# One tile for each PSUM bank, and VectorE for the two-operand work of the Strassen phases, in a kernel of attention and two feed-forward layers

## The chip, the cores and the metric

The kernel runs on one core of a Trainium2 chip, in float32. The metric is the device time of one execution in microseconds (us); the time of a kernel is the median of its runs.

## What is computed

Windowed attention over 4 x 8 heads of 768 tokens gives x of 3072 tokens by 512 features. Two feed-forward layers follow:

```python
# _moe_ref: layer 1                      # _moe2_ref: layer 2
h = x @ w_in      # 512 -> 2048          h = x @ w_in
relu6 = np.clip(h + 3.0, 0.0, 6.0)       g = np.maximum(0.01 * h, h)
g = h * relu6 / 6.0                      return g @ w_out
return g @ w_out  # 2048 -> 512
```

The inputs of the layers' weights are 64-bit floats; the kernel decodes them to 32-bit ones itself.

## The kernel before, in words

Every float32 operand is held as a high and a low part, and a product is the sum of three: high x high, low weight x high, high x low. A "low part" is a subtraction of two SBUF operands (`minus`, line 284), after the cast that makes the high part (`copy`, line 281). A matmul is 128 x 128 by 512 columns and takes one bank of PSUM.

The tokens are 6 blocks of 512. In layer 1 each block has 16 hidden blocks f (`hidden`, 12 matmuls) and 16 outputs (`output`, 12 matmuls into four banks, one for each 128 features of the result), in the order h(f+1), y(f). The outputs of layer 1 go to DRAM (`spill`).

In layer 2 the hidden products are made by Strassen's method (Winograd's form) on pairs p of blocks (2p, 2p+1) and pairs i of hidden blocks (2i, 2i+1): seven products instead of eight, each of 6 matmuls, with sums of operands before and sums of results after. `x_pair` and `x_quarter` form the right operands of a pair from `spill` (b11, t1 to t4 and others, two quarters of 11 VectorE or GpSimd operations each), `w_set` the left ones of an i (s1 to s4) from weights in DRAM, loaded into `wm`, which has two buffers; `through_dram` sends the decoded `w_out` of layer 2 through the same two buffers. `seven` makes one product and what follows from it. The order of an iteration i is products 1, 6, 5, 7, an output, products 2, 3, 4, an output; the outputs are of block 2p, from the i before. Products 2, 3 and 4 accumulate in the banks of 1, 5 and 7. The results for block 2p are used at once (`two_parts` makes g of them); those for block 2p+1 go to DRAM (`later`) and come back (`again`) when the stage is done, for an output stage of 15 or 16 outputs of block 2p+1. So there are three Strassen stages with an output stage behind each.

PSUM has eight banks. Before the change `ya` and `yb` are tiles of two banks, `h` is one of two tiles of one bank, `at` is a tile of two. Outputs and products of a stage have either `ya`, `yb` or `h`, `h`, `at`, in turn: `banks_of` gives four (tile, half) pairs. In the first and last Strassen stage products 1 and 6 write the two `h`, product 5 `at[0]`, product 7 `at[1]`, and the outputs `ya`, `yb`; in the middle stage products 1, 6, 5, 7 write `ya[0]`, `ya[1]`, `yb[0]`, `yb[1]`.

The order of all instructions is made by a planner in Python, `schedule`. A task has a key (its place in the order of TensorE's work), the engines that may do it with a cost for each, the tasks it follows, the buffers it allocates and uses. Whenever an engine is free, the planner gives it the ready task of least key and emits its instructions; a second engine of a task takes it only when the first has more than 2500 ns more to do (`SLACK`). Its costs for 512 columns are 602 ns for VectorE and 1225 for GpSimd. TensorE's products form one chain (`product`), so their order is fixed. A product is emitted in three parts of two matmuls; what reads its result is emitted some 575 ns after its planned end (`SEM` and `MARGIN`). The semaphore waits are put in afterwards by the framework, tile by tile, from the order in which the instructions were emitted. DMAs are issued by SyncE's queue, in order.

Lines that matter: 281 `copy`, 284 `minus`, 630 `hidden`'s matmuls, 684 `output`'s, 877 `seven`'s, 894 `plus` in `seven`, 905 the leak, 925 and 927 what follows product 2, 830 the sums of `w_set`, 372 and 814 the loads into `wm`, 908 and 943 the stores to `later` and the loads from it.

Of the kernel before, what the change touches and what calls it, by code (L numbers as in the profile page):

```python
# [9 lines left out]
F32 = mybir.dt.float32  # L10
# [25 lines left out]
N = 512  # L36
# [169 lines left out]
def tile_attn_moe_moe2(ctx: ExitStack, tc: tile.TileContext, raw, w1i, w1o, w2i, w2o, out):  # L206
# [15 lines left out]
    pools = {t: (ctx.enter_context(tc.tile_pool(name=t, bufs=k[0])), k[1], k[2]) for t, k in KINDS.items()}  # L222
    for y in "ab":
        pools[f"y{y}"] = (ps_y, [128, 2, 512], F32)
# [5 lines left out]
    def make(b, kind=None):  # L230
        pool, shape, dt = pools[b.tag]
# [420 lines left out]
    def banks_of(other):  # L652
        if other:
            t = Buf("at")
            return [(Buf("h"), None), (Buf("h"), None), (t, 0), (t, 1)]
        a, b = Buf("ya"), Buf("yb")
        return [(a, 0), (a, 1), (b, 0), (b, 1)]

    def bank(b):
        b, i = b  # L660
        t = made(b)
        return t if i is None else t[:, i]

    def output(lay, j, f, c0, n):
# [7 lines left out]
        banks = ybuf[lay, j]  # L672
        ys = list(dict.fromkeys(b for b, _ in banks))
        g, w = gbuf[lay, j, f, c0], wbuf[lay + "o", f]
# [30 lines left out]
    def y_out(lay, j, f, t0, n, d, y, k, two):  # L705
        s = Buf("ys")
        key = pos_y[lay, j, f] - 12
        scale = 1.0 / 6.0 if lay == "1" else 1.0
        dst = (out if lay == "2" else spill)[d, :, t0:t0 + n]
        if two and f < KF - 1:  # L710
            dst = half[j, d]

        def take(e):
            if e == "ACT":
                nc.scalar.mul(make(s)[:, :n], bank(y)[:, :n], scale)
            else:
                nc.vector.tensor_scalar(out=make(s)[:, :n], in0=bank(y)[:, :n], scalar1=scale, scalar2=None, op0=ALU.mult)

        def plus(e):
            nc.vector.scalar_tensor_tensor(out=s.t, in0=bank(y), scalar=scale, in1=s.t, op0=ALU.mult, op1=ALU.add)  # L720

        if two and f == KF - 1:
            l = add(lambda e: nc.sync.dma_start(out=make(s), in_=half[j, d]), {"SP": dma(n * 512)}, key - 8, after=[yhalf[j, d], *firsts], allocs=[s])
            k = add(plus, {"DVE": dve(n)}, key, after=[k, l], uses=[s, y[0]])
        else:
            k = add(take, {"DVE": dve(n)} if d % 2 else {"ACT": act(n, 50.0)}, key, after=[k], allocs=[s], uses=[y[0]])
# [22 lines left out]
    def x_quarter(p, j, key, need):  # L749
# [13 lines left out]
        def sub(out, x, y, after, allocs=(), uses=()):  # L763
            return add(lambda e: minus(e, out(), x(), y()), {"DVE": dve(N), "POOL": pool(N)}, key, after=after, allocs=allocs, uses=uses)

        def parts_of(name, of, own, after):
            bufs = xop[p, name]
            first = xtask[p, name][0][:1], xtask[p, name][1][:1]
            hi = add(lambda e: copy(e, operand(p, name, 0, j).bitcast(F32R), of()), {"ACT": act(N), "DVE": dve2(N)}, key, after=after + first[0], allocs=[] if first[0] else bufs[:1], uses=[own] + (bufs[:1] if first[0] else []))
            new = not first[1] and len(bufs) == 2  # L770
            lo = add(lambda e: minus(e, operand(p, name, 1, j).bitcast(F32R), of(), operand(p, name, 0, j).bitcast(F32)), {"POOL": pool(N), "DVE": dve(N)}, key, after=[hi] + first[1], allocs=bufs[1:] if new else [], uses=[own, bufs[0]] + ([] if new else bufs[1:]))
            xtask[p, name][0].append(hi)
# [19 lines left out]
        d11 = parts_of("b11", at("b11"), src["b11"], [got["b11"]])  # L792
        t1 = add(t_1, {"DVE": dve(N), "POOL": pool(N)}, key, after=[got["b11"], got["b12"]], allocs=[tt], uses=[src["b11"], src["b12"]])
        t2 = sub(t_at(1), at("b22"), t_at(0), [t1, got["b22"]], uses=[tt, src["b22"]])
# [11 lines left out]
    def w_set(p, i, key):  # L806
# [19 lines left out]
        def form(out, x, y, op, after, allocs=(), uses=()):  # L826
            def fn(e):
                for b in allocs:
                    make(b, ([128, 512], F32))
                engine(e).tensor_tensor(out=part(out), in0=part(x), in1=part(y), op=op)  # L830
            return add(fn, {"DVE": dve(256), "POOL": pool(256)}, key, after=after, allocs=allocs, uses=[*raws, *uses])

# [5 lines left out]
        def two(t, src, n, after):  # L838
# [7 lines left out]

            hi = add(fn_hi, {"ACT": act(n), "DVE": dve2(n)}, key + 0.5, after=after + gate, allocs=[ts[t]], uses=[src])
            lo = add(fn_lo, {"POOL": pool(n), "DVE": dve(n)}, key + 0.6, after=[hi], uses=[src, ts[t]])
            return hi, lo
# [6 lines left out]
    def seven(p, i, n):  # L856
# [32 lines left out]

        def plus(out, x, y, opts, after, allocs=(), uses=()):  # L890
            def fn(e):
                for q in allocs:
                    make(q, ([128, 2, N], F32) if q is ut else None)
                engine(e).tensor_tensor(out=out(), in0=x(), in1=y(), op=ALU.add)  # L894
            return add(fn, opts, key, after=after, allocs=allocs, uses=uses)

        def take(q, b, after, allocs=()):
            def fn(e):
                for x in allocs:
                    make(x, ([128, 2, N], F32))  # L900
                copy(e, ut.t[:, q], bank(b))
            return add(fn, {"ACT": act(N, 50.0), "DVE": dve(N)}, key, after=after, allocs=allocs, uses=[b[0]] + ([] if allocs else [ut]))

# [5 lines left out]

        low = {"POOL": pool(N), "DVE": dve(N)}  # L910
        dv = {"DVE": dve(N)}
        if n == 1:
            done[1] = take(0, b1, [k], allocs=[ut])
        elif n == 6:
            done[6] = plus(lambda: ut.t[:, 0], lambda: bank(b2), lambda: ut.t[:, 0], dv, [k, done[1]], uses=[ut, b2[0]])
        elif n == 5:
            done[5] = take(1, b3, [k, done[1]])
        elif n == 7:
            done[7] = plus(lambda: ut.t[:, 1], lambda: bank(b5), lambda: ut.t[:, 1], dv, [k, done[5]], uses=[ut, b5[0]])
            r = Buf("ys")  # L920
            q = plus(lambda: r.t, lambda: ut.t[:, 0], lambda: ut.t[:, 1], {"POOL": pool(N), **dv}, [done[7], done[6]], allocs=[r], uses=[ut])
            put(r, f2, leak(r, q))
        elif n == 2:
            r = Buf("r")
            q = add(lambda e: nc.scalar.mul(make(r), bank(b1), 0.01), {"ACT": act(N, 50.0)}, key, after=[k, *rs[-1:]], allocs=[r], uses=[b1[0]])
            rs.append(q)
            q = add(lambda e: nc.vector.tensor_tensor(out=r.t, in0=bank(b1), in1=r.t, op=ALU.max), dv, key, after=[q], uses=[r, b1[0]])
# [129 lines left out]
```

## Time and profile before

| | before |
|---|---|
| median of 3 runs | 1195.41 us (1194.85 to 1195.47) |
| profiled execution, its own time | 1192.55 us |
| its span in the profile | 1190.8 us |
| granted clock of TensorE, mean | 0.987 |
| last matmul ends | 1185.87 us, 4.93 us ahead of the end |
| attention and layer 1 | to about 627.7 us |
| first Strassen stage and its output stage | 627.68 to 769.57, to 813.07 us |
| middle Strassen stage and its output stage | 813.07 to 961.66, to 1004.44 us |
| last Strassen stage and its output stage | 1004.44 to 1185.87 us |

How to read it: times are us from the start of the span. PE is TensorE, DVE VectorE, ACT ScalarE, POOL GpSimd, SP SyncE's queue. A matmul's end in the profile is modelled, and matmuls overlap, so a busy share of PE is no measure of its speed: the rate of a stretch is its matmuls over its time. A VectorE instruction of 0.69 us is followed by the next about 0.60 us after its start when nothing holds that up.

### The profile page before, as it was taken

To read this page: it belongs to the slowest core of one execution; us is meant where nothing else is said; L and a number is where in the kernel's file an instruction comes from. 1 tells how busy PE (TensorE), PEld (TensorE's weight loads), DVE (VectorE), ACT (ScalarE), POOL (GpSimd) and SP (SyncE) were. 2 spreads that over 40 slices of the span, in tenths; PEclk is the share of its full clock that TensorE was granted. 3 is DMA by queue.
4 is the path that set the end of the run, shared out by engine and by line. 5 is a ranking of instruction groups with operands and counts; after the bars stand their busy time and mean duration, and the time that the engine had idled before them with its cause. 6 is when DMAs were issued, how large, how long until landed. Compare 5 with 4: busy or idle time off the path is not lost.

```text
span 1190.8 us, 19604 instructions
## 1 busy us (share of the span) xinstructions
PE 1111.6 (93%) x7632; PEld 897.2 (75%) x7632; DVE 625.4 (53%) x988; ACT 472.5 (40%) x1154; POOL 387.7 (33%) x319
## 2 busy tenths in 40 slices
PE   4599999999999999999999999899888899999998
PEld 3487888888888888888887777677666677777776
DVE  5789975554435535415517666744544571655310
ACT  4557655445554544433324333333222332322222
POOL 1030000011232232125524443664344474444343
PEclk9699999999999999999999999899999999999999
DMA  8894454654445534321103332622121260311150
GB/s 195 256 244 143 144 152 131 180 158 134 139 140 149 138 96 131 97 62 53 36 1 115 98 104 101 209 82 80 62 62 54 74 235 19 99 61 62 38 184 36
DMA packets 85341, 135.50 MB, mean 114 GB/s; under 512 B 8448, under 2 KB 41216, under 8 KB 85248
## 3 DMA queue, kind: packets, MB, share of 16 engines
q1 hardware_dynamic: 85248, 134.25, 37.3%
q8 instruction: 60, 0.98, 0.4%
q14 instruction: 33, 0.27, 0.1%
HBM read 98.57 MB, written 35.65 MB: 113 GB/s over the span
## 4 chain that ended last, share of the span: by engine, by line
PE 83%; DVE 5%; ACT 3%; DMA 3%; issue 3%; POOL 2%; SPq 2%; POOLq 0%; DVEq 0%; ACTq 0%
PE h L630 21%; PE ya L684 15%; PE yb L684 15%; PE at L877 7%; PE h L877 5%; PE h L684 5%; PE at L684 5%; PE yb L877 4%; PE ya L877 3%; ACT w L281 2%; PE at L506 1%; DMA w<-in_w1i 1%; DMA w<-in_raw 1%; PE at L445 1%; DVE ys L894 1%
## 5 line engine op out<-in xcount | busy, mean ns | idle before, releaser
L284 POOL TENSOR_TENSOR g<-r,g 128x512 fp32r<-128x512 f32 x108 | 143.2, 1326 | 463.3 <-ACT g L281 459.2
L684 PE MATMUL ya<-g,w 128*128 128x512 f32 x864 | 266.8, 394 | 4.8 <-ACT g L281 2.1
L684 PE MATMUL yb<-g,w 128*128 128x512 f32 x864 | 264.2, 391 | 0.0
L630 PE MATMUL h<-xh,w 128*128 128x512 f32 x768 | 195.5, 395 | 1.9 <-ACT xh L281 1.9
L684 PEld LDWEIGHTS ya<-g,w 128*128 128x128 f32 x864 | 160.8, 188 | 41.0 <-ACT g L281 3.5
L684 PEld LDWEIGHTS yb<-g,w 128*128 128x128 f32 x864 | 163.1, 189 | 34.8
L630 PEld LDWEIGHTS h<-xh,w 128*128 128x128 f32 x768 | 144.2, 190 | 33.1 <-ACT xh L281 3.1
L646 DVE SCALAR_TENSOR_TENSOR r<-r,h 128x512 f32<-128x512 f32 x96 | 65.9, 686 | 171.7 <-ACT r L643 171.6
L281 ACT CAST g<-r 128x512 fp32r<-128x512 f32 x144 | 89.7, 623 | 158.2 <-DVE r L646 51.4
L643 ACT ACTIVATE r<-h,three 128x512 f32<-128x512 f32 x96 | 66.6, 693 | 155.6 <-PE h L630 155.1
L630 PE MATMUL h<-xl,w 128*128 128x512 f32 x384 | 104.4, 394 | 0.6 <-issue 0.6
L684 PE MATMUL h<-g,w 128*128 128x512 f32 x288 | 89.8, 396 | 1.5 <-DVE g L284 1.0
L684 PE MATMUL at<-g,w 128*128 128x512 f32 x288 | 89.1, 394 | 0.0
L877 PE MATMUL at<-w 128*128 128x512 f32 x288 | 74.9, 398 | 14.9 <-DVE ys L894 9.4
L630 PEld LDWEIGHTS h<-xl,w 128*128 128x128 f32 x384 | 72.2, 189 | 16.2 <-issue 1.0
L284 POOL TENSOR_TENSOR g<-w,g 128x512 fp32r<-128x512 f32 x45 | 60.3, 1340 | 55.3 <-ACT g L281 55.3
L877 PEld LDWEIGHTS at<-w 128*128 128x128 f32 x288 | 52.5, 188 | 33.1 <-DVE ys L894 14.5
L684 PEld LDWEIGHTS h<-g,w 128*128 128x128 f32 x288 | 54.8, 191 | 14.6 <-DVE g L284 1.5
L281 ACT CAST g<-w 128x512 fp32r<-128x512 f32 x48 | 29.8, 621 | 85.9 <-PE at L684 55.8
L684 PEld LDWEIGHTS at<-g,w 128*128 128x128 f32 x288 | 54.9, 191 | 11.9
L284 DVE TENSOR_TENSOR w<-st,w 128x512 fp32r<-128x512 f32 x28 | 35.9, 1294 | 48.7 <-ACT w L281 48.7
L284 POOL TENSOR_TENSOR w<-wm,w 128x512 fp32r<-128x512 f32 (+1 forms) x44 | 54.8, 1250 | 8.6 <-ACT w L281 6.7
(163 smaller groups left out, 1502.0 us busy)
## 6 DMA issues: line engine op xcount, KB each, us to landing
wm<-w322i SPq DMA_DIRECT2D x48, 256.0 KB
later<-ys SPq DMA_DIRECT2D x48, 256.0 KB
w<-later SPq DMA_DIRECT2D x24, 512.0 KB
a<-in_raw SPq DMA_DIRECT2D x44, 224.0 KB
w<-in_w1i SPq DMA_DIRECT2D x16, 512.0 KB
w<-in_w1o SPq DMA_DIRECT2D x16, 512.0 KB
w<-in_w2i SPq DMA_DIRECT2D x16, 512.0 KB
w<-in_w2o SPq DMA_DIRECT2D x16, 512.0 KB
```

The costliest lines, as they stand in the source:

```text
L281: nc.scalar.copy(out, in_) if e == "ACT" else engine(e).tensor_copy(out=out, in_=in_)
L284: engine(e).tensor_tensor(out=out, in0=a, in1=b, op=ALU.subtract)
L445: nc.tensor.matmul(ps.t[h * CHUNK:(h + 1) * CHUNK, par, i * W:(i + 1) * W], qk[h // 2].t[r, gp, (h % 2) * G + c * CHUNK:(h % 2) * G + (c + ...
L506: nc.tensor.matmul(pv.t[(h % 2) * D:(h % 2 + 1) * D, par, (h // 2) * 2 * G + i * CHUNK:(h // 2) * 2 * G + (i + 1) * CHUNK], v[h // 2].t[r, ...
L630: nc.tensor.matmul(h.t[:, :n], w.t[:, 1 if p == 1 else 0, k * 128:(k + 1) * 128], x[:, k, c0:c0 + n], start=(p == 0 and k == 0), stop=(p = ...
L643: nc.scalar.activation(out=make(r)[:, :n], in_=h.t[:, :n], func=AF.Relu, bias=three[:, 0:1], scale=1.0)
L646: nc.vector.scalar_tensor_tensor(out=r.t[:, :n], in0=r.t[:, :n], scalar=6.0, in1=h.t[:, :n], op0=ALU.min, op1=ALU.mult)
L684: nc.tensor.matmul(bank(banks[d])[:, c0:c0 + n], w.t[:, 1 if p == 1 else 0, d * 128:(d + 1) * 128], g.t[:, 1 if p == 2 else 0, :n], start= ...
L877: nc.tensor.matmul(bank(to), t.t[:, 1 if q == 1 else 0, o, kt * 128:(kt + 1) * 128], operand(p, name, 1 if q == 2 else 0, kt).bitcast(F32R ...
L894: engine(e).tensor_tensor(out=out(), in0=x(), in1=y(), op=ALU.add)
```

## The change

Each of the eight banks gets a tile of its own. `ya` and `yb` become four tiles `y`; `at` becomes, when attention is done, two tiles `hx`; before the first output, where units of attention had `ya` and `yb`, they have tiles `ab` and `ac`, whose pool is closed when the first `y` is made. `banks_of` gives four tiles.

In `x_quarter`, `w_set`, `seven`, `again` and for the g of layer 2 the choice of engine goes: every subtraction and sum is VectorE's, every cast of a high part there ScalarE's. `split_w` and `hidden` keep theirs (GpSimd makes layer 1's low parts of g from the third block on).

After the products the sums are ordered anew. Before: U2 = P1 + P6 (P1 copied by ScalarE), P5 copied by ScalarE, P5 + P7 with P7 in PSUM, and then U2 + (P5 + P7), both in SBUF, by GpSimd or VectorE. After: U3 = P5 + U2 with P5 in PSUM, then P7 + U3 with P7 in PSUM, both by VectorE.

```diff
-    ps_y = ctx.enter_context(tc.tile_pool(name="ps_y", bufs=1, space=PSUM))
     ps_h = ctx.enter_context(tc.tile_pool(name="ps_h", bufs=2, space=PSUM))
-    ps_a = ctx.enter_context(tc.tile_pool(name="ps_a", bufs=1, space=PSUM))
+    begin = ctx.enter_context(ExitStack())
+    ps_b = begin.enter_context(tc.tile_pool(name="ps_b", bufs=1, space=PSUM))
+    attention = ctx.enter_context(ExitStack())
+    ps_a = attention.enter_context(tc.tile_pool(name="ps_a", bufs=1, space=PSUM, side="right"))
...
-    places |= {"ya": 1, "yb": 1, "h": 2, "at": 1}
+    places |= {"ab": 1, "ac": 1, "y": 4, "h": 2, "at": 1, "hx": 2}
...
+        if b.tag in ("hx", "y") and b.tag not in pools:
+
+            (attention if b.tag == "hx" else begin).close()
...
     def banks_of(other):
-        if other:
-            t = Buf("at")
-            return [(Buf("h"), None), (Buf("h"), None), (t, 0), (t, 1)]
-        a, b = Buf("ya"), Buf("yb")
-        return [(a, 0), (a, 1), (b, 0), (b, 1)]
+        return [Buf(t) for t in (("h", "h", "hx", "hx") if other else "yyyy")]
...
-            hi = add(lambda e: copy(e, operand(p, name, 0, j).bitcast(F32R), of()), {"ACT": act(N), "DVE": dve2(N)}, key, after=after + first[0], allocs=[] if first[0] else bufs[:1], uses=[own] + (bufs[:1] if first[0] else []))
+            hi = add(lambda e: copy(e, operand(p, name, 0, j).bitcast(F32R), of()), {"ACT": act(N)}, key, after=after + first[0], allocs=[] if first[0] else bufs[:1], uses=[own] + (bufs[:1] if first[0] else []))
...
-            lo = add(fn_lo, {"POOL": pool(n), "DVE": dve(n)}, key + 0.6, after=[hi], uses=[src, ts[t]])
+            hi = add(fn_hi, {"ACT": act(n)}, key + 0.5, after=after + gate, allocs=[ts[t]], uses=[src])
+            lo = add(fn_lo, {"DVE": dve(n)}, key + 0.6, after=[hi], uses=[src, ts[t]])
...
-        low = {"POOL": pool(N), "DVE": dve(N)}
-        dv = {"DVE": dve(N)}
+        low = {"DVE": dve(N)}
...
-            done[5] = take(1, b3, [k, done[1]])
+            done[5] = plus(lambda: ut.t[:, 1], lambda: bank(b3), lambda: ut.t[:, 0], [k, done[6]], uses=[ut, b3])
         elif n == 7:
-            done[7] = plus(lambda: ut.t[:, 1], lambda: bank(b5), lambda: ut.t[:, 1], dv, [k, done[5]], uses=[ut, b5[0]])
             r = Buf("ys")
-            q = plus(lambda: r.t, lambda: ut.t[:, 0], lambda: ut.t[:, 1], {"POOL": pool(N), **dv}, [done[7], done[6]], allocs=[r], uses=[ut])
-            put(r, f2, leak(r, q))
+            done[7] = plus(lambda: r.t, lambda: bank(b5), lambda: ut.t[:, 1], [k, done[5]], allocs=[r], uses=[ut, b5])
+            put(r, f2, leak(r, done[7]))
...
-        two_parts("2", 2 * p + 1, f, r, k, key, {"POOL": pool(N), "DVE": dve(N)}, f % 2)
+        two_parts("2", 2 * p + 1, f, r, k, key, {"DVE": dve(N)}, f % 2)
...
-        unit(u // 2, u % 2, -80.0 + 6.0 * u, ("at", "ya", "yb", "at")[u], own=u < 3, direct=True)
+        unit(u // 2, u % 2, -80.0 + 6.0 * u, ("at", "ab", "ac", "at")[u], own=u < 3, direct=True)
```

## Rows read from the trace of the kernel before

**Rows 1.** The page: busy us (share of the span) and instructions of each engine.

```profile
PE 1111.6 (93%) x7632; PEld 897.2 (75%) x7632; DVE 625.4 (53%) x988; ACT 472.5 (40%) x1154; POOL 387.7 (33%) x319
```

**Rows 2.** Chain of waits in order of time (start, us, what), one iteration, first stage.

```profile
640.90 2.72 PE h L877 x12
643.62 1.83 PE at L877 x8
...
645.47 0.59 ACT w L281
...
653.24 0.70 DVE ys L894
...
657.93 2.72 PE h L877 x12
```

**Rows 3.** Waits of TensorE, 560 to 1190: who for whom: us, times, longest.

```profile
PE at L877 <- ACT w L281: 10.9, 16, 0.8
PE at L877 <- DVE ys L894: 9.4, 12, 0.8
PE yb L877 <- DVE ys L894: 6.7, 7, 2.0
PE yb L877 <- ACT w L281: 5.4, 8, 0.7
PE ya L877 <- ACT w L281: 5.3, 7, 0.8
```

**Rows 4.** Busy us (instructions) by stage: stretch, us, engines, granted clock, DMA, GB/s.

```profile
627.68:769.57 141.89, 129.30 (x542) 101.64 (x541) 98.62 (x130) 53.39 (x97) 66.78 (x50) 0.98 0.37 123
769.57:813.07 43.50, 42.16 (x182) 34.18 (x181) 15.40 (x15) 14.79 (x26) 26.73 (x20) 0.98 0.26 84
813.07:961.66 148.59, 131.02 (x541) 100.70 (x541) 80.30 (x119) 41.21 (x75) 65.74 (x50) 0.99 0.26 85
961.66:1004.44 42.78, 41.42 (x181) 33.63 (x181) 15.64 (x15) 14.27 (x25) 25.81 (x19) 1.00 0.28 100
1004.44:1185.87 181.43, 170.53 (x732) 135.89 (x731) 73.28 (x106) 45.55 (x80) 74.73 (x59) 1.00 0.23 77
```

**Rows 5.** Waits of TensorE again, of the last stretch alone, 1004.44 to 1185.87.

```profile
PE at L877 <- DVE ys L894: 5.5, 7, 0.8
PE at L877 <- ACT w L281: 5.4, 8, 0.7
```

**Rows 6.** Timeline of TensorE, end of the first stage: start, us, what [idle before <-releaser].

```profile
763.13 0.73 PE L684 MATMUL ya<-g,w 128*128 128x512 f32 x2 [1.77 <-ACT g L281]
764.94 2.07 PE L684 MATMUL ya<-g,w 128*128 128x512 f32 x4 [1.07 <-POOL g L284]
```

**Rows 7.** Busy us by stretch, as rows 4: layer 1's end; the first stage's end.

```profile
585.00:640.00 55.00, 54.23 (x238) 44.28 (x237) 19.50 (x26) 16.76 (x28) 18.27 (x14) 1.00 0.09 29
735.00:810.00 75.00, 69.02 (x285) 54.61 (x284) 40.47 (x43) 25.52 (x45) 43.22 (x30) 0.95 0.41 134
```

**Rows 8.** Tile wm, 600 to 760: instructions, ns of one (min/median/max), first and last start.

```profile
L284 DVE TENSOR_TENSOR w<-wm,w x18: 679/686/1523, 637.3 to 743.3; 128x512 fp32r<-128x512 f32 x16, 128x256 fp32r<-128x256 f32 x2
```

**Rows 9.** Groups by shape, 560 to 1190: busy us, mean ns, idle before: VectorE, then GpSimd.

```profile
L284 DVE TENSOR_TENSOR w<-st,w 128x512 fp32r<-128x512 f32 x28 | 35.9, 1294 | 48.7 <-ACT w L281 48.7
...
L894 DVE TENSOR_TENSOR w<-at,w 128x512 f32<-128x512 f32 x16 | 11.1, 692 | 21.8 <-PE at L877 21.0 <-ACT w L281 0.8
...
L284 POOL TENSOR_TENSOR g<-r,g 128x512 fp32r<-128x512 f32 x57 | 74.3, 1303 | 197.6 <-ACT g L281 193.5 <-issue 4.1
```

**Rows 10.** Timeline of VectorE and of GpSimd at the end of the first stage.

```profile
752.37 1.77 DVE L284 TENSOR_TENSOR w<-a 128x512 f32<-128x512 f32 x1
...
751.86 1.73 POOL L284 TENSOR_TENSOR w<-a,w 128x512 fp32r<-128x512 f32 x1
```

**Rows 11.** Timeline of SyncE's queue and of ScalarE: a load into wm and its cast.

```profile
680.05 1.07 SPq L372 DMA_DIRECT2D wm<-w322o  x2
...
683.12 0.62 ACT L281 CAST w<-wm 128x512 fp32r<-128x512 f32 x1 [1.62 <-DMA wm<-w322o]
```

More of the change, by code (lines that the diff above doesn't have):

```diff
@@ L222, in tile_attn_moe_moe2 @@
     pools = {t: (ctx.enter_context(tc.tile_pool(name=t, bufs=k[0])), k[1], k[2]) for t, k in KINDS.items()}
-    for y in "ab":
-        pools[f"y{y}"] = (ps_y, [128, 2, 512], F32)
+    for a in "bc":
+        pools[f"a{a}"] = (ps_b, [128, 2, 512], F32)
     pools["h"] = (ps_h, [128, 512], F32)
@@ L227, in tile_attn_moe_moe2 @@
     places = {t: k[0] for t, k in KINDS.items()}
-    places |= {"ya": 1, "yb": 1, "h": 2, "at": 1}
+    places |= {"ab": 1, "ac": 1, "y": 4, "h": 2, "at": 1, "hx": 2}
     def make(b, kind=None):
+        if b.tag in ("hx", "y") and b.tag not in pools:
+            (attention if b.tag == "hx" else begin).close()
+            pools[b.tag] = (ctx.enter_context(tc.tile_pool(name=b.tag, bufs=places[b.tag], space=PSUM, side="right" if b.tag == "hx" else "left")), [128, 512], F32)
         pool, shape, dt = pools[b.tag]
@@ L672, in output @@
         banks = ybuf[lay, j]
-        ys = list(dict.fromkeys(b for b, _ in banks))
+        ys = banks
         g, w = gbuf[lay, j, f, c0], wbuf[lay + "o", f]
@@ L723, in y_out @@
             l = add(lambda e: nc.sync.dma_start(out=make(s), in_=half[j, d]), {"SP": dma(n * 512)}, key - 8, after=[yhalf[j, d], *firsts], allocs=[s])
-            k = add(plus, {"DVE": dve(n)}, key, after=[k, l], uses=[s, y[0]])
+            k = add(plus, {"DVE": dve(n)}, key, after=[k, l], uses=[s, y])
         else:
-            k = add(take, {"DVE": dve(n)} if d % 2 else {"ACT": act(n, 50.0)}, key, after=[k], allocs=[s], uses=[y[0]])
+            k = add(take, {"DVE": dve(n)} if d % 2 else {"ACT": act(n, 50.0)}, key, after=[k], allocs=[s], uses=[y])
         k = add(lambda e: nc.sync.dma_start(out=dst, in_=s.t[:, :n]), {"SP": dma(n * 512)}, key, after=[k], uses=[s])
@@ L763, in sub @@
         def sub(out, x, y, after, allocs=(), uses=()):
-            return add(lambda e: minus(e, out(), x(), y()), {"DVE": dve(N), "POOL": pool(N)}, key, after=after, allocs=allocs, uses=uses)
+            return add(lambda e: minus(e, out(), x(), y()), {"DVE": dve(N)}, key, after=after, allocs=allocs, uses=uses)
         def parts_of(name, of, own, after):
@@ L768, in parts_of @@
             first = xtask[p, name][0][:1], xtask[p, name][1][:1]
-            hi = add(lambda e: copy(e, operand(p, name, 0, j).bitcast(F32R), of()), {"ACT": act(N), "DVE": dve2(N)}, key, after=after + first[0], allocs=[] if first[0] else bufs[:1], uses=[own] + (bufs[:1] if first[0] else []))
+            hi = add(lambda e: copy(e, operand(p, name, 0, j).bitcast(F32R), of()), {"ACT": act(N)}, key, after=after + first[0], allocs=[] if first[0] else bufs[:1], uses=[own] + (bufs[:1] if first[0] else []))
             new = not first[1] and len(bufs) == 2
-            lo = add(lambda e: minus(e, operand(p, name, 1, j).bitcast(F32R), of(), operand(p, name, 0, j).bitcast(F32)), {"POOL": pool(N), "DVE": dve(N)}, key, after=[hi] + first[1], allocs=bufs[1:] if new else [], uses=[own, bufs[0]] + ([] if new else bufs[1:]))
+            lo = add(lambda e: minus(e, operand(p, name, 1, j).bitcast(F32R), of(), operand(p, name, 0, j).bitcast(F32)), {"DVE": dve(N)}, key, after=[hi] + first[1], allocs=bufs[1:] if new else [], uses=[own, bufs[0]] + ([] if new else bufs[1:]))
             xtask[p, name][0].append(hi)
@@ L792, in x_quarter @@
         d11 = parts_of("b11", at("b11"), src["b11"], [got["b11"]])
[L793 removed]
+        t1 = add(t_1, {"DVE": dve(N)}, key, after=[got["b11"], got["b12"]], allocs=[tt], uses=[src["b11"], src["b12"]])
         t2 = sub(t_at(1), at("b22"), t_at(0), [t1, got["b22"]], uses=[tt, src["b22"]])
@@ L830, in fn @@
                 engine(e).tensor_tensor(out=part(out), in0=part(x), in1=part(y), op=op)
-            return add(fn, {"DVE": dve(256), "POOL": pool(256)}, key, after=after, allocs=allocs, uses=[*raws, *uses])
+            return add(fn, {"DVE": dve(256)}, key, after=after, allocs=allocs, uses=[*raws, *uses])
         s1 = form("s1", "a21", "a22", ALU.add, l, allocs=sums[:1])
@@ L870, in seven @@
         xb, (xhi, xlo) = xop[p, name], xtask[p, name]
-        alloc = [to[0]] if fresh and n != 7 and not (n == 6 and to[1] is not None) else []
+        alloc = [to] if fresh else []
         need = [done[{2: 1, 3: 5, 4: 7}[n]]] if n in THEN else []
@@ L888, in seven, with plus @@
         pk[p, i, n] = k
-        def plus(out, x, y, opts, after, allocs=(), uses=()):
+        def plus(out, x, y, after, allocs=(), uses=()):
             def fn(e):
                 for q in allocs:
[L893 to L902, printed above, removed]
+                    make(q)
+                nc.vector.tensor_tensor(out=out(), in0=x(), in1=y(), op=ALU.add)
+            return add(fn, {"DVE": dve(N)}, key, after=after, allocs=allocs, uses=uses)
         def leak(r, after):
@@ L908, in put, with take @@
             held["b", p, f] = add(lambda e: nc.sync.dma_start(out=later[p, f], in_=r.t), {"SP": dma(N * 512)}, key, after=[after], uses=[r])
[L910 to L911 removed]
+        low = {"DVE": dve(N)}
         if n == 1:
[L913 removed]
+            def take(e):
+                make(ut, ([128, 2, N], F32))
+                copy(e, ut.t[:, 0], bank(b1))
+            done[1] = add(take, {"ACT": act(N, 50.0)}, key, after=[k], allocs=[ut], uses=[b1])
         elif n == 6:
[L915 removed]
+            done[6] = plus(lambda: ut.t[:, 0], lambda: bank(b2), lambda: ut.t[:, 0], [k, done[1]], uses=[ut, b2])
         elif n == 5:
[L917 removed]
+            done[5] = plus(lambda: ut.t[:, 1], lambda: bank(b3), lambda: ut.t[:, 0], [k, done[6]], uses=[ut, b3])
         elif n == 7:
[L919 removed]
             r = Buf("ys")
[L921 to L922 removed]
+            done[7] = plus(lambda: r.t, lambda: bank(b5), lambda: ut.t[:, 1], [k, done[5]], allocs=[r], uses=[ut, b5])
+            put(r, f2, leak(r, done[7]))
         elif n == 2:
             r = Buf("r")
[L925 removed]
+            q = add(lambda e: nc.scalar.mul(make(r), bank(b1), 0.01), {"ACT": act(N, 50.0)}, key, after=[k, *rs[-1:]], allocs=[r], uses=[b1])
             rs.append(q)
[L927 removed]
+            q = add(lambda e: nc.vector.tensor_tensor(out=r.t, in0=bank(b1), in1=r.t, op=ALU.max), {"DVE": dve(N)}, key, after=[q], uses=[r, b1])
             two_parts("2", a, f1, r, q, key, low)
@@ L930, in seven @@
             r = Buf("ys")
-            q = plus(lambda: r.t, lambda: bank(b3), lambda: ut.t[:, 0], dv, [k, done[6]], allocs=[r], uses=[ut, b3[0]])
+            q = plus(lambda: r.t, lambda: bank(b3), lambda: ut.t[:, 0], [k, done[6]], allocs=[r], uses=[ut, b3])
             put(r, f1, leak(r, q))
@@ L934, in seven @@
             r = Buf("r")
-            q = plus(lambda: r.t, lambda: bank(b5), lambda: ut.t[:, 0], dv, [k, done[6], *rs[-1:]], allocs=[r], uses=[ut, b5[0]])
+            q = plus(lambda: r.t, lambda: bank(b5), lambda: ut.t[:, 0], [k, done[6], *rs[-1:]], allocs=[r], uses=[ut, b5])
             rs.append(q)
```

7 lines of the change are left out of this document (2 added, 5 removed).

## The prediction, made before the change was run

> **What bounds the kernel now.** I began with the engines' busy row: TensorE is busy 93% of the span and no other engine over 53% [rows 1]. So the question is what TensorE waits for, and where. The chain of waits in order of time shows it. One iteration of the first Strassen stage runs from 640.90 to 657.93 us, 17.03 us, and twice TensorE stops inside a product: after 8 matmuls on `at` it stands until ScalarE has finished a copy, then again until VectorE has finished a sum [rows 2]. Neither is an operand. Product 5 writes `at[0]` and product 7 writes `at[1]`; the first two matmuls of product 7 run, then the copy of `at[0]` is emitted, and the rest of product 7 waits for that reader of the other half. Products 3 and 4 do the same with the sum. Products 1 and 6, which have a tile each (`h`), don't wait in this stage; in the middle stage they share `ya`, and there they do: 7 waits "ya <- ACT" [rows 3]. The waits go with sharing a tile, not with the data.
>
> **What a wait costs.** Twelve matmuls take 2.72 us when nothing holds them [rows 2], 0.2267 each. An iteration has 7 products of 6 matmuls and two outputs of 12, 66 in all: 14.96 us. Each stage is measured against its matmuls in this way [rows 4]; a Strassen stage has 8 x 42 + 17 x 12 = 540 (122.4 us), the output stages between have 15 x 12 = 180 (40.8 us), the last stretch 540 + 192 = 732 (165.9 us).
> - first stage 141.89, excess 19.5
> - outputs between 43.50, excess 2.7
> - middle stage 148.59, excess 26.2
> - outputs between 42.78, excess 2.0
> - last stretch 181.43, excess 15.5
>
> Together 65.9 us. The list has 16 + 12 + 7 + 8 + 7 = 50 waits of this kind [rows 3]: the 22 on `ya` and `yb` are the middle stage's, and of the 28 on `at` the last stretch has 7 + 8 = 15 [rows 5], the first stage 13. The last stretch has no other waits: 15.5 / 15 = 1.035 us each (the idle time of some 0.7 plus the refill of the pipeline). At that price the 50 are worth **51.8 us**, and 65.9 - 51.8 = **14.1 us** is something else: 6.0 in the first stage, 3.4 in the middle one, 4.7 in the output stages.
>
> **The other 14.1 us** lie at the ends of the first two Strassen stages and in the outputs after them. There `x_pair` forms the next pair's operands, while the last products need their results; the last stage has no next pair and no such loss. In the timeline an output waits 1.77 us for a cast and 1.07 us for GpSimd's low part, and the matmuls after that take about twice their time [rows 6]; the granted clock of that stretch is 0.95, that is, a part of it ran at the lower of the two levels, 1.2 of 2.4 GHz [rows 7], against 1.00 in the last stretch, where there are only the short waits [rows 4]. VectorE and GpSimd hold each other up: a subtraction with two SBUF operands takes VectorE 0.69 us at the median and 1.52 at most [rows 8], 1.29 on the mean for `w<-st` [rows 9], and 1.77 beside a GpSimd instruction of 1.73 [rows 10].
>
> The Trainium skill (SBUF — State Buffer, Who interferes with whom) says that a VectorE instruction with two SBUF inputs and a GpSimd instruction that reads SBUF shut each other out for a whole instruction, and one with a PSUM input doesn't. The trace bears it out: 0.692 us on the mean of 16 sums with a PSUM operand, whose stages have GpSimd at work too [rows 4, 9]. The rule speaks against the change in one place, the end of layer 1, where GpSimd keeps its low parts and VectorE is given more; that is priced below from rows.
>
> **The change, part by part.**
> (1) *A tile for each bank.* All 50 waits named above lose their cause: -51.8 us. True orders stay. Product 3 must follow the reader of product 5, product 4 that of product 7, product 2 that of product 1, and each bank's next product its last reader. With iteration time 0 at product 1, product 7 ends at 5.44, product 4 starts at 10.88: 5.4 us of cover for one 0.69 us sum. The next iteration's product 1 starts 5.4 us after product 2 ends, which covers ScalarE's 0.6 and VectorE's 0.69. For layer 1's outputs nothing changes: I find no such wait there. The initial pools only hold attention units; zero.
> (2) *The combination.* 24 ScalarE copies of product 5 (0.59 each, as in [rows 2]) and the sum on GpSimd (a two-operand instruction of this size takes it about 1.3 us [rows 9]) go. VectorE does three sums with a PSUM operand instead of two: +24 x 0.69. All beside TensorE's work: zero on the path, unless VectorE is full. Product 5's sum now needs product 6's first; that one comes 1.36 us earlier and costs no wait.
> (3) *GpSimd's work to VectorE.* Per iteration VectorE then has 6 operations with a PSUM operand (0.692 us), 8 of 512 with two SBUF operands (three leaks, two low parts of g, three of weights), and 5 of half size, at half price: 6 x 0.69 + 10.5 x 0.69 = 11.4 us of 14.96. The first stage adds two low parts of `w_out`: 12.8 us. VectorE is filled to 76 and 86%; the weights' burst (3 low parts, 5 halves) is 5.5 x 0.69 = 3.8 us and fits into the 5.4 us of cover. Queued behind it on VectorE are the leaks, and behind those, on SyncE, the stores to `later` and then the next weight loads; all are used about an iteration later. In an output stage VectorE has 15 low parts, 22 of `x_pair` and the first weights: about 29 us of 40.8. So GpSimd's removal costs nothing on the path, and at the transitions it takes away the stretching from 0.69 to 1.77. From below it returns none of the 14.1 us (VectorE now has what both did: in a last iteration and its two outputs, 14.96 + 5.44 = 20.4 us, 11 operations of the products, 11 of `x_pair` and up to 6 for weights, 28 x 0.69 = 19.3 us), from above all. I take 10: the planner puts the last products' work ahead of `x_pair`'s by its key, so the urgent work waits for one operation at most, and the lower clock came after the long waits only.
> (4) *End of layer 1, 560 to 627 us.* GpSimd keeps one low part (1.3 us [rows 9]) in each hidden block and output, 24 matmuls or 5.44 us; VectorE gets all of `x_pair`. Now TensorE idles 0.8 us in it [rows 7]. If every one of some 11 GpSimd instructions holds VectorE up by 1.77 - 0.69 = 1.08 us, that is 12 us of VectorE's time, 1.08 us in each 5.44; an output begins 5.44 us after the hidden block it belongs to and reads the low part in its last third, so most of that is covered. Bounds: 0.8 us gained, 5 us lost. I take 0.
>
> **Sum:** 51.8 + 10 = 62 us. The profiled execution, 1192.55 us (span 1190.8), would become 1130.5; it lies 2.9 us under the median of the timed runs, 1195.41, so the median becomes **1134 us** (rounded up). Everything returned, with the 0.8, would be 66.7: 1128.7. With nothing of the 14.1 and 5 us lost at layer 1's end: 1148.6.
>
> **Rivals.**
> *A, a loading chain paces the first stage (1140 to 1160 us).* Weights of both layers go through two `wm` buffers there. An issue at 680.05 lets its cast start at 683.12 [rows 11]: 3.1 us per load, some 0.5 more for the second of two issued together. Two rounds of load, cast, low part and forms: 3.6 + 1.4 + 3.6 + 1.6, some 10 us, up to 13 with queues on VectorE, against 14.96. If queues make it 17, the first stage keeps its old pace and its 13.5 us: 1134 + 13.5 = 1148; with lateness at the transitions, 1160. For it: now the cycle fits the 17.03 us closely. Against: it waits there for product 1 of each iteration, so the period sets it, not the loads.
> *B, VectorE becomes the bound (slower, about 1230 us).* This needs the two-operand time to stay stretched without GpSimd. With x us per operation, 24 iterations take 24 x 4.1 + (8 x 12.5 + 16 x 10.5) x = 98.4 + 268 x. TensorE's 359 us are reached at x = 0.97; the present 359 + 51.8 = 411 at x = 1.17. At the mean of 1.29 [rows 9]: 444, 33 us more than now: about 1229. Against it: the median of 0.686 us [rows 8] in the same stage.
> *C, the waits stay (about 1185 us).* If it isn't the shared tile but an order of the engines, only the 10 us of (3) come. Against: the contrast of `h` and `ya`.
>
> **How the numbers follow.** The forecast, with its own bounds 1128 to 1149: 0.76. A: 0.12. C: 0.04, of which half within 0.2%, when VectorE eats up the 10 us. B: 0.06, and 0.02 for other slowing. The range must leave out 2 in 10 at most: 1128 to 1158 holds the forecast's bounds and most of A. A change within 0.2% (2.4 us) is about what a measurement of this kernel can't tell from none. Faster 0.90, same 0.02, slower 0.08.
>
> **What would show it.** Right: no wait of products (L877 of before) for ScalarE's copies or VectorE's sums; product 1 to product 1 in 15.0 us; Strassen stages of 123 to 126 us; GpSimd nearly idle after layer 1; VectorE's two-operand instructions at 0.69 throughout. (3) is wrong if outputs still wait for g at the transitions and the clock falls there; A shows as products or outputs waiting for the weights' casts or low parts; B as VectorE busy without gaps; C as the same 50 waits on other tiles. A planner that orders VectorE's queue otherwise than I assume would make the 10 us wrong in either direction.

## The result, and the profile after

The changed kernel takes 1128.8 us, against 1195.1 us for the kernel before: a ratio of 0.945 (95% interval 0.9425 to 0.9475). Run once more beside other kernels it took 1124.6 us, ratio 0.942 (0.940 to 0.9445). The forecast was 1134 us, the range 1128 to 1158: right in sign and in its main term, 5 us too slow, and near the lower end of its own range; the second time, 1124.6 us, lies 3 us below that range. The profiled execution took 1129.08 us, its span 1127.2.

Line numbers move with the edits. The subtraction `minus` is L284, L288, L290 or L295; the copies are L281, L285, L287 or L289; the products are L877, L880, L882 or L886; the sums behind them are L894, L897, L901 or L903.

The page of the changed kernel gives busy us, share and instructions by engine, and then groups of instructions (busy us, mean ns, idle before):

```profile
PE 1090.8 (97%) x7632; PEld 899.6 (80%) x7632; DVE 672.7 (60%) x1180; ACT 467.7 (41%) x1146; POOL 110.8 (10%) x111
...
L684 PE MATMUL y<-g,w 128*128 128x512 f32 x1728 | 416.7, 390 | 0.0
...
L877 PE MATMUL hx<-w 128*128 128x512 f32 x288 | 69.2, 389 | 0.0
```

TensorE waits 0.0 us before the products into the new tiles; [rows 3] had 50 waits there, and the list of TensorE's waits from the first Strassen product on is now empty. The chain of waits in order of time, for the iteration that answers to [rows 2], holds nothing but matmuls:

```profile
643.43 2.72 PE h L877 x12
646.15 2.72 PE hx L877 x12
648.87 2.72 PE y L684 x12
651.59 1.36 PE h L877 x6
652.95 2.72 PE hx L877 x12
655.67 2.72 PE y L684 x12
658.39 2.72 PE h L877 x12
```

From product 1 to product 1 it is 658.39 - 643.43 = 14.96 us instead of 17.03. The stages, with the columns of [rows 4]:

```profile
631.03:753.50 122.47, 122.47 (x542) 101.45 (x541) 100.53 (x174) 49.27 (x90) 0.99 (x1) 1.00 0.42 137
753.50:794.30 40.80, 40.80 (x182) 33.80 (x181) 22.43 (x40) 16.00 (x29) 0.00 (x0) 1.00 0.30 105
794.30:916.74 122.44, 122.44 (x542) 101.42 (x541) 90.89 (x159) 39.09 (x72) 0.00 (x0) 1.00 0.31 103
916.74:957.50 40.76, 40.76 (x182) 33.76 (x181) 21.14 (x37) 14.91 (x27) 0.00 (x0) 1.00 0.30 105
957.50:1123.40 165.90, 165.90 (x733) 137.18 (x731) 94.27 (x159) 43.88 (x78) 0.00 (x0) 1.00 0.25 84
```

Each stage lasts as long as its matmuls, at the full clock (2.4 GHz) throughout; [rows 4] and [rows 7] had 0.98 and 0.95 where the stage ended in long waits. VectorE (the third engine) is busy 82% of the first stage, and GpSimd (the fifth) has one instruction there and none afterwards. VectorE's groups by shape (mean ns after the bar) answer to [rows 9]:

```profile
L290 DVE TENSOR_TENSOR w<-st,w 128x512 fp32r<-128x512 f32 x48 | 30.9, 684 | 0.0
...
L894 DVE TENSOR_TENSOR w<-hx,w 128x512 f32<-128x512 f32 x16 | 11.0, 687 | 1.8 <-PE hx L877 1.8
```

The same subtraction that took 1294 ns on the mean takes 684, as much as the sum with a PSUM operand.

There is also a gain at the very end that the prediction did not look at. In the timelines of the kernel before and, behind it, of the changed one, these are the last two reads of output banks:

```profile
1185.89 0.69 DVE L717 TENSOR_SCALAR ys<-at 128x512 f32<-128x512 f32 x1 [0.67 <-PE at L684]
1186.62 0.60 ACT L715 ACTIVATE ys<-at 128x512 f32<-128x512 f32 x1 [2.17 <-DVE ys L717]
...
1122.87 0.60 ACT L715 ACTIVATE ys<-hx 128x512 f32<-128x512 f32 x1 [0.76 <-PE hx L684]
1123.55 0.69 DVE L717 TENSOR_SCALAR ys<-hx 128x512 f32<-128x512 f32 x1 [0.67 <-PE hx L684]
```

With one tile for two banks ScalarE's read came after VectorE's; with two tiles it comes while TensorE still fills the other bank. From the last matmul's end to the end of the span it is 3.65 us instead of 4.91. With `at` alone split it is 3.65 too, and with VectorE and the new sums alone 4.92.

### The profile page after: what moved, and what is told of

It reads as the page before. It is cut to its first block, busy times and chain, and to the rows that moved or that the text cites. A ratio compares the mean times of both kernels' runs of the same rounds, so it can differ in the third digit from the quotient of the medians.

```text
span 1127.2 us, 19446 instructions
## 1 busy us (share of the span) xinstructions
PE 1090.8 (97%) x7632; PEld 899.6 (80%) x7632; DVE 672.7 (60%) x1180; ACT 467.7 (41%) x1146; POOL 110.8 (10%) x111
## 4 chain that ended last, share of the span: by engine, by line
PE 93%; DMA 3%; SPq 2%; DVE 1%; ACT 1%; issue 0%; DVEq 0%
PE y L684 35%; PE h L636 23%; PE hx L877 8%; PE y L877 7%; PE hx L684 6%; PE h L684 6%; PE h L877 6%; PE at L512 2%; DMA w<-in_w1i 1%; PE at L451 1%; SPq L416 1%; DMA w<-in_raw 1%; PE at L501 1%; DMA w<-in_w1o 1%; SPq L427 0%
## 5 line engine op out<-in xcount | busy, mean ns | idle before, releaser
L684 PE MATMUL y<-g,w 128*128 128x512 f32 x1728 | 416.7, 390 | 0.0
L684 PEld LDWEIGHTS y<-g,w 128*128 128x128 f32 x1728 | 323.2, 188 | 67.5
L652 DVE SCALAR_TENSOR_TENSOR r<-r,h 128x512 f32<-128x512 f32 x96 | 65.9, 686 | 169.3 <-ACT r L649 169.0
L287 ACT CAST g<-r 128x512 fp32r<-128x512 f32 x144 | 90.1, 626 | 132.2 <-DVE r L652 48.5
L290 POOL TENSOR_TENSOR g<-r,g 128x512 fp32r<-128x512 f32 x64 | 88.0, 1376 | 324.9 <-ACT g L287 320.2
L684 PE MATMUL hx<-g,w 128*128 128x512 f32 x288 | 87.7, 389 | 0.0
L290 DVE TENSOR_TENSOR g<-w,g 128x512 fp32r<-128x512 f32 x48 | 33.1, 690 | 68.3 <-ACT g L287 68.3
L290 DVE TENSOR_TENSOR g<-r,g 128x512 fp32r<-128x512 f32 x80 | 56.4, 705 | 22.8 <-ACT g L287 22.5
L877 PE MATMUL hx<-w 128*128 128x512 f32 x288 | 69.2, 389 | 0.0
L287 ACT CAST g<-w 128x512 fp32r<-128x512 f32 x48 | 30.0, 625 | 84.6 <-PE hx L684 51.7
L290 DVE TENSOR_TENSOR w<-wm,w 128x512 fp32r<-128x512 f32 x88 | 54.5, 622 | 15.9 <-ACT w L287 15.9
L877 PEld LDWEIGHTS hx<-w 128*128 128x128 f32 x288 | 54.1, 188 | 11.2
L684 PEld LDWEIGHTS hx<-g,w 128*128 128x128 f32 x288 | 54.1, 188 | 11.2
L287 ACT CAST w<-wm 128x512 fp32r<-128x512 f32 x88 | 48.5, 561 | 11.4 <-DVE wm L355 11.1
```

Of the source, the lines that this page charges most:

```text
L287: nc.scalar.copy(out, in_) if e == "ACT" else engine(e).tensor_copy(out=out, in_=in_)
L290: engine(e).tensor_tensor(out=out, in0=a, in1=b, op=ALU.subtract)
L652: nc.vector.scalar_tensor_tensor(out=r.t[:, :n], in0=r.t[:, :n], scalar=6.0, in1=h.t[:, :n], op0=ALU.min, op1=ALU.mult)
L684: nc.tensor.matmul(bank(banks[d])[:, c0:c0 + n], w.t[:, 1 if p == 1 else 0, d * 128:(d + 1) * 128], g.t[:, 1 if p == 2 else 0, :n], start= ...
L877: nc.tensor.matmul(bank(to), t.t[:, 1 if q == 1 else 0, o, kt * 128:(kt + 1) * 128], operand(p, name, 1 if q == 2 else 0, kt).bitcast(F32R ...
```

## The experiments

Two numbers are read from each: the median, and the stretch in TensorE's timeline from the start of the first Strassen product to the start of the last matmul, plus the time of one. The stretch leaves out the start of the kernel, which varies by some us. Its matmuls alone are 2172 x 0.22667 = 492.3 us, so what is over is TensorE's loss. Numbers in brackets behind a median are its ratio to the kernel before, timed beside it (1192.1 to 1193.7 us), and the 95% interval.

| kernel | median us | stretch us | over 492.3 |
|---|---|---|---|
| before | 1195.1 | 558.2 | 65.9 |
| changed; run again | 1128.8; 1124.6 | 492.3; 492.3 | 0; 0 |
| own tiles alone | 1143.2 | 510.8 | 18.5 |
| VectorE and new sums alone | 1159.5 | 526.0 | 33.7 |
| `at` alone split | 1162.6 | 529.1 | 36.8 |
| own tiles and new sums, GpSimd kept | 1144.9 | 512.7 | 20.4 |
| changed, old sums; run again | 1124.6; 1125.1 | 492.3; 492.3 | 0; 0 |
| changed, operands to GpSimd again | 1138.8 | 506.3 | 14.0 |
| changed, g to GpSimd again | 1126.5 | 494.1 | 1.8 |
| changed, idle work on GpSimd | 1168.6 | 536.1 | 43.8 |
| changed, 4 pairs added on VectorE | 1127.8 | 495.2 | 2.9 |
| changed, 10 pairs added on VectorE | 1216.5 | 583.6 | 91.3 |

**Own tiles alone.** The changed kernel with the engines and sums of before (two places of the edit):

```diff
-            done[5] = plus(lambda: ut.t[:, 1], lambda: bank(b3), lambda: ut.t[:, 0], [k, done[6]], uses=[ut, b3])
+            done[5] = add(lambda e: copy(e, ut.t[:, 1], bank(b3)), {"ACT": act(N, 50.0), "DVE": dve(N)}, key, after=[k, done[1]], uses=[ut, b3])
...
-        low = {"DVE": dve(N)}
+        low = {"POOL": pool(N), "DVE": dve(N)}
```

> Only the tiles of the banks are changed; the engines and the order of the sums are those of before. Theory (two separate causes): the 50 waits on shared tiles go, 51.8 us, and the 14 us at the transitions stay, since VectorE and GpSimd still share the work: about 1143 us; the Strassen stages at 128, 126 us, the last stretch at its 165.9. Rival 1 (the faster TensorE leaves less cover, so the same contention costs more): over 1150 us, with waits for g or for the sums inside the iterations. Rival 2 (the transitions' loss was a follow-up of the waits): 1129 to 1133 us.

It took 1143.2 us (ratio 0.958, 0.956 to 0.960): the 50 waits are gone and the loss at the transitions is not. What remains are waits of outputs for g. Three of the eight, in TensorE's timeline at the end of the first stage and just after it, the first two as in [rows 6]:

```profile
749.32 0.73 PE L684 MATMUL y<-g,w 128*128 128x512 f32 x2 [1.77 <-ACT g L287]
751.12 4.15 PE L684 MATMUL y<-g,w 128*128 128x512 f32 x10 [1.07 <-POOL g L290]
770.87 0.73 PE L684 MATMUL h<-g,w 128*128 128x512 f32 x2 [2.88 <-DVE g L290]
```

The third was 1.05 us in the kernel before. The transitions cost 18.5 us instead of 14.1, so Rival 1 holds to a small part; that the faster TensorE leaves less cover is its reason as argued, not shown by itself.

**VectorE and the new sums alone**, with the shared tiles of before:

> Only the engines and the order of the sums are changed; the banks share tiles as before. Theory: the waits on shared tiles stay, each 1.04 us or 0.1 more where VectorE's sum of 0.69 takes the place of ScalarE's copy of 0.59, and the transitions' 14 us go: 1181 to 1185 us. Rival (the transitions' loss comes of the waits): 1193 us or more.

Both were wrong: 1159.5 us (0.972, 0.970 to 0.9745), a gain of 34 us. TensorE's waits (who for whom, us, times, longest) say why:

```profile
PE at L877 <- DVE ys L894: 10.2, 13, 0.8
PE yb L877 <- DVE ys L894: 5.5, 7, 0.8
PE ya L877 <- ACT w L281: 4.7, 7, 0.7
PE at L877 <- DVE w L894: 2.4, 3, 0.8
PE yb L877 <- DVE w L894: 0.8, 1, 0.8
```

They are 31, not 50, and 31 x 1.035 = 32.1 us is nearly all of its 33.7: no output waits at a transition any more, and 20 of the 24 waits for the reader of product 5 (`w` in the lines with `at` and `yb`) are gone although products 5 and 7 share a tile. In TensorE's timeline one product 7 runs through (12 matmuls with product 5) and the next one waits:

```profile
641.64 2.88 PE L877 MATMUL at<-w 128*128 128x512 f32 x12
...
657.72 1.98 PE L877 MATMUL at<-w 128*128 128x512 f32 x8
660.48 1.20 PE L877 MATMUL at<-w 128*128 128x512 f32 x4 [0.78 <-DVE w L894]
```

and VectorE's timeline has the two sums that read product 5:

```profile
645.39 0.69 DVE L894 TENSOR_TENSOR w<-at,w 128x512 f32<-128x512 f32 x1
...
659.73 0.69 DVE L894 TENSOR_TENSOR w<-at,w 128x512 f32<-128x512 f32 x1 [0.46 <-PE at L877]
```

The first stood in VectorE's queue and came after product 7; the second came at once, between product 7's matmuls. A reader makes the rest of the other product wait only if it is emitted between its parts. ScalarE read product 5 between the parts of product 7 in all 24 iterations; VectorE does in 4. Here the reader's engine was changed together with the order of the sums, so which of the two makes it later is not shown.

**`at` alone split**, the kernel before with two tiles `hx` for products 5 and 7:

```diff
-            t = Buf("at")
-            return [(Buf("h"), None), (Buf("h"), None), (t, 0), (t, 1)]
+            return [(Buf(t), None) for t in ("h", "h", "hx", "hx")]
```

> As before, but the tile of two banks used by products 5 and 7 in the first and last Strassen stage is two tiles. Theory: exactly the 28 waits on it go, 29 us, and the 22 of the middle stage stay: 1166 us; the last stretch at 166 us, the middle stage still at 148.6. Rival (the waits come of the order of the engines, not of the shared tile): 1193 us or more, the waits on the new tiles.

1162.6 us (0.975, 0.973 to 0.9775), in the stretch 29.1 us less, the 29 expected. The waits on `at` are gone, and those of the middle stage are there as in [rows 3]:

```profile
PE yb L880 <- DVE ys L897: 6.7, 7, 2.0
PE yb L880 <- ACT w L285: 5.4, 8, 0.7
PE ya L880 <- ACT w L285: 5.3, 7, 0.8
```

22 x 1.035 + 14.1 = 36.9 us of loss; the table has 36.8. The waits belong to the shared tile: that is shown.

**Own tiles and new sums, GpSimd kept:**

> As the changed kernel, but with the choice of GpSimd given back for low parts and subtractions; the new order of the sums stays (no sum of two SBUF operands after product 7). Theory: the contention of the low parts makes the transitions' loss, so it stays as in the kernel with new tiles alone: 1140 to 1145 us. Rival (the sum of two SBUF operands on GpSimd was what held the last products up): 1129 to 1133 us.

1144.9 us (0.959, 0.957 to 0.962), as with the tiles alone. The sum that GpSimd loses is not what held the last products up.

**The old order of the sums, the rest as changed**, alone and once more beside the changed kernel:

> As the changed kernel (own tiles, VectorE alone), but with the old order of the sums: product 5 copied by ScalarE, and a sum of two SBUF operands after product 7, on VectorE. Theory (the order of the sums lies wholly beside TensorE's work, VectorE having 0.6 us less to do in an iteration or more makes no difference): 1127 to 1131 us, no excess over the matmuls in the three Strassen stages. Rival (the new order is what frees the banks in time): 1131 us and more, waits of products.

> The kernel with own tiles, VectorE alone and the old order of the sums, beside the changed one on the same chip. Theory: no difference between the two, within 0.2%. Rival: this one is faster by about 0.3%, as the medians of the two earlier comparisons seem to say.

> The changed kernel once more, beside the one with the old order of the sums. Theory (the first 60 us differ between executions and chips, all else is the same): the same gapless stretch of 492.4 us from the first Strassen product to the last matmul; the start of the first product within 626 to 632 us; 1124 to 1130 us.

1124.6 us (0.9425, 0.941 to 0.944), then 1125.1 beside 1124.6 us for the changed kernel. The stretch is 492.3 us in all of them. With own tiles and VectorE alone the order of the sums is worth nothing; the first difference of 4 us was one of the start (the first Strassen product at 631.0 against 626.5 us).

**Which of GpSimd's work costs time.** First only the operands of the next pair, then only layer 2's g have the choice of GpSimd again:

> As the changed kernel, but only the operands of the next pair have the choice of GpSimd again; g, the weights and all sums stay with VectorE. Theory (GpSimd beside VectorE stretches VectorE's instructions, and the operands of the next pair are what stretches them at the transitions): most of the 14 us is lost again, 1137 to 1143 us, with outputs waiting for VectorE's low parts of g. Rival (GpSimd's own low parts of g, 1.3 us instead of 0.69, are what comes late): 1128 to 1132 us.

> The other half: as the changed kernel, but only the low parts of layer 2's g have the choice of GpSimd again. Theory (contention with the operands): little is lost, 1129 to 1133 us, as GpSimd then has one instruction in each output only. Rival (late low parts of g on GpSimd): 1137 to 1143 us, with outputs waiting for GpSimd.

1138.8 us (0.954, 0.952 to 0.9565) and 1126.5 us (0.944, 0.942 to 0.946). With the operands back, the loss is 14.0 us, and the waits are for ScalarE's and VectorE's part of g, none for GpSimd; with g back it is 1.8 us (its median lies under the expected 1129 us because it was reckoned from 1128.8, where the run again has 1124.6). GpSimd's own slowness is not the cause, VectorE's being held up is. With the operands back, the longest wait of the first transition can be followed through the timelines of GpSimd, VectorE, ScalarE and TensorE, one behind the other:

```profile
744.70 1.75 POOL L290 TENSOR_TENSOR xl<-a,xl 128x512 fp32r<-128x512 f32 x1
746.41 1.74 POOL L290 TENSOR_TENSOR w<-a,w 128x512 fp32r<-128x512 f32 x1
...
745.22 1.77 DVE L290 TENSOR_TENSOR g<-r,g 128x512 fp32r<-128x512 f32 x1
746.92 1.77 DVE L898 SCALAR_TENSOR_TENSOR ys<-ys 128x512 f32<-128x512 f32 x1
749.55 0.68 DVE L898 SCALAR_TENSOR_TENSOR r<-r 128x512 f32<-128x512 f32 x1
...
750.34 0.62 ACT L287 CAST g<-r 128x512 fp32r<-128x512 f32 x1 [4.08 <-DVE r L898]
...
751.00 0.73 PE L684 MATMUL y<-g,w 128*128 128x512 f32 x2 [2.38 <-ACT g L287]
```

Two VectorE operations of 1.77 us beside GpSimd's stand ahead of the leak that makes r; the cast of r waits for the leak, and the output waits for the cast.

**Idle work on GpSimd** makes the same point without any dependence on it (two of the three places where the work is added are left out):

```diff
+    junk = const.tile([128, 256], F32, name="junk")
+    def idle_sum(engine_, cost, key, after):
+        add(lambda e: [minus(e, junk, junk, junk) for _ in range(2)], {engine_: cost}, key, after=after)
...
             hi = add(fn_hi, {"ACT": act(n)}, key + 0.5, after=after + gate, allocs=[ts[t]], uses=[src])
             lo = add(fn_lo, {"DVE": dve(n)}, key + 0.6, after=[hi], uses=[src, ts[t]])
+            idle_sum("POOL", pool(N), key + 0.6, [hi])
```

> As the changed kernel, with work added that nobody waits for: beside each low part of layer 2 GpSimd makes two subtractions of 256 columns in a scratch tile, about the time of its low parts before. Theory (an instruction of two SBUF operands on either engine holds up one on the other): VectorE's two-operand instructions go from 0.69 to 1.2 us and more on the mean, those with a PSUM operand stay at 0.69; with 6 such additions in an iteration of 1.08 us each VectorE's 11.4 us become 17.9 and TensorE waits: 1160 to 1210 us. Rival (VectorE's long instructions came of its own operands, not of GpSimd): 1127 to 1131 us, 0.69 us as in the changed kernel.

1168.6 us (0.9795, 0.977 to 0.981). GpSimd's work was waited for by nobody, and GpSimd was done with it at 1016 us, so one execution holds both cases. By stretch, with the columns of [rows 4]:

```profile
627.56:997.40 369.84, 339.76 (x1440) 271.17 (x1439) 325.50 (x405) 117.97 (x216) 337.79 (x411) 0.99 0.31 103
1000.00:1162.00 162.00, 162.00 (x716) 134.13 (x716) 95.75 (x157) 42.35 (x76) 14.48 (x21) 1.00 0.25 83
```

The first holds 1440 matmuls, 326.4 us of work, so 43.4 us are lost in it and none in the second. VectorE's groups of 630 to 990 us, and behind them those of 1020 to 1160 us:

```profile
L295 DVE TENSOR_TENSOR g<-r,g 128x512 fp32r<-128x512 f32 x32 | 31.9, 996 | 5.1 <-ACT g L289 4.6
...
L295 DVE TENSOR_TENSOR w<-st,w 128x512 fp32r<-128x512 f32 x32 | 28.8, 939 | 0.0
...
L903 DVE TENSOR_TENSOR ys<-hx,w 128x512 f32<-128x512 f32 x16 | 10.8, 678 | 0.2
...
L295 DVE TENSOR_TENSOR g<-r,g 128x512 fp32r<-128x512 f32 x14 | 9.7, 690 | 5.9 <-ACT g L289 5.9
...
L295 DVE TENSOR_TENSOR w<-st,w 128x512 fp32r<-128x512 f32 x10 | 6.4, 683 | 0.0
```

Subtractions of two SBUF operands take 0.94 to 1.0 us beside GpSimd, 0.68 to 0.69 without; the sum with a PSUM operand (`ys<-hx,w`) takes 0.68 even beside GpSimd. The stretching is less than the 1.2 us expected. GpSimd's instructions of 256 columns are shorter here, by its group over 630 to 990 us:

```profile
L295 POOL TENSOR_TENSOR junk<-junk 128x256 f32<-128x256 f32 x400 | 329.5, 824 | 31.3
```

They take 0.82 us on the mean where those of 512 columns took 1.3 [rows 9]; that this is why VectorE loses less is likely, but was not tried.

**When VectorE becomes the bound.** Work that nobody waits for is added on VectorE in each iteration. What the texts call an addition is a pair of subtractions of 256 columns in a scratch tile, `junk`:

> As the changed kernel, with 4 additions of two halves of 256 columns on VectorE in each Strassen iteration, in a scratch tile, that nobody waits for. Theory (VectorE is beside the path until it is full; counted from start to start, 0.60 us for 512 columns and 0.33 for 256, it has 10.1 us of 14.96 to do, 11.3 in the first stage, and these add 2.7): no change, the changed kernel's time within 0.3%.

> The same with 10 additions, 6.7 us: VectorE then has 16.8 us to do of 14.96, 18.0 in the first stage. Theory (then VectorE is the bound): 16 x 1.8 + 8 x 3.0 = 53 us slower than the changed kernel, about 1180 us. Rival (TensorE's waits set in earlier or later than a full VectorE): the 4 additions cost time already, or the 10 cost nothing.

Four cost 3 us (1127.8 us; 0.944, 0.942 to 0.946), within the 0.3% of the expectation but not nothing, since two waits of 1.4 and 0.2 us appear; ten make it 1216.5 us (1.018, 1.015 to 1.021), slower than the kernel before. With ten, VectorE is full; busy us by stretch (third engine) and two starts of product 1 in TensorE's timeline:

```profile
680.00:700.00 20.00, 16.67 (x67) 13.32 (x66) 19.59 (x41) 5.74 (x10) 1.28 (x1) 0.91 0.24 79
```

```profile
683.43 1.52 PE L882 MATMUL h<-xh,w 128*128 128x512 f32 x6
...
703.61 1.52 PE L882 MATMUL h<-xh,w 128*128 128x512 f32 x6
```

An iteration takes 20.2 us. The size was off: an addition costs more than the 0.67 us expected, by VectorE's timeline

```profile
680.81 0.88 DVE L295 TENSOR_TENSOR junk<-junk 128x256 f32<-128x256 f32 x2
681.60 0.68 DVE L929 TENSOR_TENSOR r<-h,r 128x512 f32<-128x512 f32 x1
```

0.79 us from start to start (681.60 - 680.81). Ten are 7.9, so by this count VectorE has 11.3 + 7.9 = 19.2 us to do in the first stage and 18.0 in the others: 8 x 4.2 + 16 x 3.0 = 82 us of the 91 lost. The granted clock is 0.91 in the 20 us shown and 0.96 over the whole stretch, so a part of both ran at the lower level (1.2 GHz), with waits of up to 3.6 us in it; how much of the loss belongs to the clock was not separated.

## Why the prediction was right, and where its numbers were off

(1) *A tile for each bank, 51.8 us.* Right. Alone it gave 50 us by the medians and 47.4 of the stretch (558.2 - 510.8): 51.8 less the 4.4 us by which the transitions grew. That the waits come of the shared tile was read from the contrast of `h` and `ya`, and `at` alone bears it out. What the prediction did not see is that the wait also needs a reader that is emitted early; it doesn't change the sum, since own tiles take away both, but the second experiment was mispriced for it by some 20 us. It also left out the 1.3 us at the end of the kernel, which are own tiles' too.

(2) *The new sums, zero.* Right with own tiles: 492.3 us with either order.

(3) *GpSimd's work to VectorE, 10 of 14.1 us.* This term was mis-sized: all 14.1 us came back, 18.5 us counted from the kernel with own tiles, where it had grown. The prediction feared that VectorE, with 28 operations in 20.4 us, would still be late. It isn't: in the last 20.4 us of the first stage it is busy 18.1 us, in those of the middle stage 16.7, and no output waits. The mechanism, instructions of two SBUF operands held up by GpSimd's, is shown by the work that nobody waits for.

(4) *End of layer 1, taken as zero.* Right, but its upper bound of 0.8 us was a misreading. The row of [rows 7] runs to 640 us, past the first Strassen product at 627.5, and the idle time in it is a wait inside a product, already one of the 50 of (1):

```profile
632.89 1.19 PE L877 MATMUL at<-w 128*128 128x512 f32 x4 [0.68 <-ACT w L281]
```

From 560 to 627 us the kernel before has 66.9 busy us of 67.0, so nothing was to be gained there, and "everything returned" is 65.9 us, not 66.7. In the changed kernel TensorE is busy 46.0 of the 46.0 us from 585 to 631: GpSimd's low parts stretch a few of VectorE's subtractions there, up to 1.79 us, and TensorE waits for none of them.

So the changes account for 65.9 us in the stretch and 1.3 at the end, where the prediction had 62. What one comparison shows depends on the start as well. The profiled execution gained only 63.5 us, which is 65.9 + 1.3 less the 3.5 by which its first Strassen product came later, but for rounding: that began at 631.0 us, in the other profiled executions of this study between 626.0 and 628.8, and in the kernel before at 627.5. The medians fell by 66.3 us, and by 69.1 when it was run again. That the first of them lies so close to the 66.7 and inside the range, and the second below it, is chance of the start.

Rival A (the loads) did not show: no wait in the first stage is for the weights' casts, at 14.96 us an iteration. Rival B's condition did not hold: VectorE's operations stayed at 0.68 to 0.69 us without GpSimd. A full VectorE does become the bound, but not near: about 3 us more in an iteration cost 3 us in all, 8 us more cost 91. Rival C fell with `at` alone. No version was found that beats the changed kernel: the others at 492.3 us equal it, and that stretch holds nothing but matmuls.

## What to carry to other kernels

Give every PSUM bank a tile of its own where several readers empty several banks: a matmul into one half of a tile waited for a reader of the other half, 0.7 us of idle time and 1.04 us of lost time at each of 50 places, and a reader waited for the reader of the other half at the end. An engine that "helps" can slow down the one it helps: count what an instruction takes beside the other engine's, not alone (1.77 against 0.69 us here). And before all of its work is moved to one engine, add up what that engine then has to do in an iteration, by start to start: here 10.1 to 11.3 us of 14.96, and some 3 us of room.

## What the runs showed of the hardware

VectorE's sums with one operand in PSUM and with both in SBUF take the same time when GpSimd is quiet: 687 and 684 ns. Beside GpSimd's subtractions only the latter grow: 678 against 939 ns in one and the same stretch. GpSimd is held up too: 1.74 and 1.75 us beside VectorE's for what took 1.30 on the mean [rows 9]. Two VectorE instructions of 256 columns that work in place on the same tile take 0.79 us from start to start of what follows, where independent ones of that size were counted at 0.33 each. The start of the kernel, up to the first Strassen product, differed by up to 5 us between two executions of the changed kernel (631.0 and 626.0 us); what decides it was not tried.
